# A new table of steps for a fused RWKV-5 and squared-ReLU FFN kernel: seven loads issued by ScalarE's queue, two more chunks transposed on TensorE

## The chip, the cores and the metric

The kernel runs on one core of one Trainium2 chip. The metric is the device time of one execution in microseconds, lower is better. Three runs of the kernel before took 174.09, 176.03 and 176.28 us (median 176.03 us). One further execution was recorded by the hardware profiler; every line of profile below comes from it.

## The reference

Two layers follow each other. The first is a linear attention with a decayed state, per batch `b` (4) and head `h` (8), over 768 time steps, with heads of width 48; the second is a feed-forward layer on the 3072 rows of width 384 that come out of it.

```python
for t in range(S):
    kt, vt, rt = (k[:, :, t].copy(), v[:, :, t].copy(), r[:, :, t].copy())
    cur = np.einsum('bhd,bhe->bhde', u[None] * kt, vt)
    y[:, :, t] = np.einsum('bhd,bhde->bhe', rt, state + cur)
    state = w[None, :, :, None] * state + np.einsum('bhd,bhe->bhde', kt, vt)
...
x = np.ascontiguousarray(attn_out.transpose(0, 2, 1, 3)).reshape(B * S, H * D)
h = np.maximum(x @ w_in, 0.0)          # w_in 384 x 2048
return (h * h @ w_out)                 # w_out 2048 x 384
```

All inputs and the output are float32 in HBM; the matmuls of the kernel work on bf16.

## The kernel before

**Tiling.** The 3072 rows are 24 chunks of 128 time steps; chunk `i` is batch `i % 4` and part `i // 4` of the sequence. Chunks 0 to 9, 22 and 23 go through the feed-forward layer one by one, the others in pairs (a "unit" `n` is one chunk or one pair; unit 15 is the last pair, 16 and 17 are chunks 22 and 23).

**Steps.** Each piece of work is a step with a short key, and a function `do_...` that issues its instructions:

- `Lr`, `Lk`, `Lv` + chunk (line 313): one DMA of 192 KB that loads r, k or v of the chunk. `wrow`, `urow` (263, 266) load the small rows w and u.
- `ln`, `bw`, `exk`, `ext`, `wt`, `wl`, `bu`, `ub` (274 to 302) make the powers of the decay, `Wkhat` and `Wt2`, once. `wlm` (304) spreads the last of them.
- `kh`, `rt` (327, 330) scale k and r; `P0`, `P`, `du`, `dv` (333 to 353) make the term with u; `vb` (355) casts v to bf16.
- `Tk`, `Tr` (371, 374): four TensorE transposes each of the scaled k and r, evicted by `ek`, `er` (377, 380). From chunk 5 on one DMA transpose `T` (383) on SyncE's queue does the work of both.
- `A` (388): 8 matmuls of scores; `M` (404): mask and eviction; `Y` (414): 8 matmuls, and 4 more against the state from chunk 4 on; `U`, `S` (431, 446): state update; `xs`, `X`, `xT` (441, 452, 459): sum, transpose (3 matmuls) and eviction into the layout of the feed-forward layer.
- `W1_q`, `W2_q` (476): one DMA of 768 KB for a quarter `q` of `w_in` or `w_out`. It goes into one of 5 float32 staging tiles and is cast to bf16 by `C1_q`, `C2_q` (484). `W2_3` alone is issued by GpSimd's queue, with the cast in the DMA.
- `F n_s` (489): 12 matmuls (6 of twice the width for a pair) of hidden units; `F n_q` of a single chunk needs quarter `q` of `w_in`. `R`, `Q` (506, 512): relu, then square. `G i_q` (523): 4 matmuls of output that need quarter `q` of `w_out`. `os`, `st` (541, 554): eviction and store.

**Order.** A table, `ORDER` (line 25), the written-out result of a search, lists all 915 steps as `key:engine`, with P for TensorE, A for ScalarE, D for VectorE, G for GpSimd, S for SyncE, and behind P the numbers of the PSUM banks. `Plan.run` (117) reads it, and the loop at line 575 issues the steps in this order. The scheduler is switched off (`tc.manual_schedule()`), so each engine runs its own steps strictly in the order in which the table lists them, and waits only for data, tiles and banks. All loads and all weight quarters but `W2_3` are issued by SyncE. `preload_act_table_set` (205) is ScalarE's first instruction. `PE_T` (17) is a constant that no other line reads; the number of chunks transposed on TensorE follows from the table.

In the table before, SyncE's list begins: `Lr0 wrow Lr1 Lk0 Lk1 urow Lr2 Lk2 Lk3 Lr3 Lv1 Lv0 Lv2 W1_0 W1_1 Lv3 Lk4 Lr4 W1_2 W1_3 Lv4 Lk5 Lr5 W2_0 W2_1 Lv5 Lk6 T5 W2_2 Lr6 Lr7 Lk7`. TensorE's list around the first output steps reads: `... F2_2 F1_3 F4_1 F4_3 U4 F4_0 G0_0 G3_0 G2_0 G3_1 G0_1 A5 F4_2 G1_0 G2_1 U5 Y5 G1_1 G4_0 G1_2 G2_2 X5 G3_2 ...`. `C2_0` and `C2_1` are cast by GpSimd, `C2_2` by ScalarE.

Of the kernel before, what the change touches and what calls it, by code (L numbers as in the profile page):

```python
# [25 lines left out]
Lr0:S wrow:S ln:A bw:P0 exk:A ext:A Lr1:S Lk0:S Lk1:S P00:D P01:D wt:P1 wl:A kh0:D kh1:D rt0:D  # L26
urow:S Lr2:S bu:P0 ub:A Tk0:P1 ek0:A Lk2:S kh2:D Tr0:P2 rt1:D Lk3:S P02:D kh3:D rt2:D er0:A Tk2:P0
Tr1:P1 er1:A Tk1:P2 ek1:A ek2:A A0:P34 Tk3:P1 A1:P25 Tr2:P0 Lr3:S Lv1:S Lv0:S vb0:A ek3:A vb1:A
er2:A P0:D M0:D du0:D M1:D rt3:G P1:G Lv2:S W1_0:S du1:D Tr3:P6 er3:A vb2:A C1_0:A W1_1:S Lv3:S
Lk4:S Lr4:S W1_2:S W1_3:S Lv4:S Lk5:S Lr5:S W2_0:S W2_1:S Lv5:S Lk6:S dv0:G P03:G dv1:G Y0:P3  # L30
xs0:D U0:P4 U1:P1 A2:P07 M2:D Y1:P2 A3:P56 X0:P3 xs1:D X1:P0 xT0:A F0_0:P2 wlm:D P2:G P3:G du2:D
du3:D dv2:G xT1:A F1_0:P0 Y2:P3 C1_1:A dv3:G kh4:G rt4:G vb3:A F1_1:P7 R1_0:A R0_0:A M3:D Y3:P5
xs2:D U3:P0 U2:P6 X2:P3 F0_1:P2 S1:D xs3:D xT2:D X3:P5 Tk4:P1 S0:D F2_1:P3 Tr4:P4 xT3:D S2:D S3:D
er4:D ek4:D F3_0:P5 F2_0:P6 F3_1:P0 Q1_0:A R1_1:A Q1_1:G P04:G P4:G R0_1:A Q0_1:D A4:P14 Q0_0:A
C1_2:A F0_2:P7 F3_2:P2 R3_0:A Q3_0:D M4:D du4:D W2_3:G dv4:G kh5:G rt5:G T5:S C1_3:A F3_3:P5
F2_3:P1 R3_1:A vb4:A Y4:P4 Q3_1:D R3_2:A Q3_2:D F0_3:P0 F1_2:P2 xs4:D X4:P4 R2_0:A R2_3:A Q2_0:D
R2_1:A R0_2:A Q2_3:A xT4:A Q2_1:D F2_2:P1 W2_2:S R2_2:A R3_3:A Q0_2:A Q3_3:D F1_3:P6 R0_3:A Q2_2:A
Q0_3:A F4_1:P4 vb5:A R4_1:A R1_3:A F4_3:P1 R4_3:A Q4_1:A R1_2:A C2_0:G U4:P3 F4_0:P7 S4:D G0_0:P0
G3_0:P5 G2_0:P3 C2_1:G G3_1:P G0_1:P A5:P16 M5:D F4_2:P4 G1_0:P2 G2_1:P R4_0:A Q1_2:A Q4_0:A
C2_2:A P05:G kh6:G P5:G du5:D dv5:D Lr6:S rt6:G U5:P1 Y5:P6 xs5:D S5:D G1_1:P G4_0:P7 G1_2:P  # L40
G2_2:P Lr7:S Lk7:S X5:P1 G3_2:P G2_3:P Q1_3:A R4_2:A Q4_3:A os2:A xT5:D F5_0:P1 G3_3:P os3:A
G0_2:P Lr8:S Lv6:S vb6:A F5_1:P3 T6:S A6:P54 Lk8:S rt7:G kh7:G T7:S rt8:D P06:D P6:D du6:D P07:G
kh8:G dv6:G M6:D G0_3:P os0:D G4_1:P F5_3:P6 R5_1:A R5_0:A Q5_0:A Y6:P4 P08:D xs6:D U6:P0 A7:P51
F5_2:P3 X6:P4 G1_3:P Q4_2:A G4_2:P M7:D G5_0:P1 Lv7:S vb7:A xT6:A Y7:P4 Lk9:S Lr9:S T8:S F6_0:P5
G4_3:P P7:G du7:D P8:G du8:D kh9:G dv7:D xs7:D X7:P4 rt9:G P09:D Q5_1:A os1:A R5_3:A Q5_3:A G5_1:P
A8:P62 S6:D M8:D Lv9:S Lv8:S Lr11:S Lk11:S Lr10:S R6_0:A xT7:A P9:G Q6_0:G R5_2:A F6_2:P4 R6_2:A
F6_3:P3 R6_3:A Q5_2:A vb8:A F7_2:P0 U7:P4 F7_3:P2 R7_3:A F7_0:P3 Q6_3:A R7_0:A G5_2:P Y8:P2 du9:D
dv8:D S7:D xs8:D F7_1:P4 F6_1:P3 X8:P2 xT8:D Lk10:S G5_3:P T9:S G6_0:P6 A9:P25 Q6_2:A vb9:A R6_1:A
Q7_3:A Q6_1:A st0:S Lr12:S Lv10:S rt10:G kh10:G T10:S rt11:G st1:S Lk12:S F8_2:P3 Q7_0:A R7_1:A
R7_2:A G6_1:P P010:D kh11:D M9:D F8_1:P4 Y9:P0 U9:P2 F8_3:P5 R8_2:A Q7_2:A R8_1:A Q7_1:A G6_2:P  # L50
G7_0:P3 vb10:A os5:A P10:D dv9:G du10:D xs9:D X9:P0 xT9:A R8_3:A T11:S Q8_2:A F8_0:P1 G7_1:P
R8_0:A F9_2:P0 Lv11:S Lk14:S Lk13:S Lr13:S Lk15:S P011:G P11:G dv10:G os4:D Q8_1:D S9:D P012:D
rt12:G st2:S Lv12:S st3:S kh12:G P12:G T12:S du11:D dv11:G rt13:G kh13:G P013:G A10:P52 M10:D
A11:P47 M11:D R9_2:A F9_3:P1 F9_0:P0 G7_2:P vb11:A R9_3:A Q9_3:A Q8_3:A Q8_0:A U8:P1 F9_1:P2
R9_1:A R9_0:A Q9_0:A Y10:P4 S8:D xs10:D Y11:P7 xs11:D du12:D U11:P5 G7_3:P G6_3:P X10:P7 G8_0:P0
X11:P4 Q9_2:A xT10:A xT11:A S11:D G9_0:P2 U10:P7 P13:D S10:D kh14:G dv12:D du13:D G8_1:P F10_7:P4
F10_6:P5 F10_1:P7 T13:S Lr15:S R10_7:A kh15:G Q10_7:G rt15:G os7:A R10_1:A Q10_1:D Q9_1:A os6:D
F10_0:P4 F10_2:P3 G8_2:P G9_1:P R10_0:A R10_2:A vb12:A st5:S Lr14:S P014:G P14:G Lv13:S dv13:G
rt14:G Q10_2:D vb13:A A12:P64 A13:P71 M12:D M13:D R10_6:A Q10_6:A Q10_0:A G8_3:P G9_2:P F10_3:P3
R10_3:A Q10_3:A G9_3:P Y12:P5 Y13:P1 os9:D xs12:D F10_5:P7 G11_0:P2 xs13:D X13:P1 X12:P5 xT12:D  # L60
Lk16:S st4:S Lr17:S st7:S F10_4:P3 G10_0:P4 U12:P5 xT13:D F11_2:P1 F11_3:P6 R10_4:A R10_5:A
Q10_5:A R11_3:A Q10_4:A P015:G Lr16:S P016:D os8:D S12:D Q11_3:D du14:D rt16:G rt17:G P15:G du15:D
Lv15:S Lv14:S vb14:A T14:S T15:S F11_1:P0 U13:P5 F11_7:P7 R11_1:A G11_1:P vb15:A F11_0:P6 G11_2:P
G10_1:P R11_2:A Q11_2:A R11_0:A Lk17:S Lr18:S S13:D A14:P51 A15:P03 dv14:G P16:D kh16:G M14:D
dv15:G Q11_1:A R11_7:A G10_2:P U15:P6 G11_3:P F11_5:P1 M15:D F11_4:P5 Y15:P0 Q11_7:D os11:D
Q11_0:G kh17:G P017:G Y14:P3 xs14:D F11_6:P7 R11_6:A Q11_6:G G10_3:P X14:P3 U14:P2 xT14:A R11_5:A
R11_4:A xs15:D X15:P0 xT15:D du16:D G12_0:P7 G13_0:P3 F12_4:P1 G13_1:P F12_0:P5 Q11_4:A F12_1:P0
R12_0:A st6:S st9:S Lk18:S Lr19:S Lv16:S Lk19:S kh19:G T16:S Lk21:S os10:A rt18:G S15:D S14:D
rt19:D P17:D Q11_5:A R12_4:A vb16:A F12_3:P2 G12_1:P F12_2:P4 G12_2:P Q12_0:D kh18:G dv16:G T17:S
Lv17:S st8:S A17:P56 Q12_4:D du17:D R12_3:A R12_1:A Lk20:S Lr20:S T18:S T19:S Lr21:S P018:D dv17:G  # L70
P019:G kh20:G A16:P21 M16:D G13_2:P F12_5:P0 vb17:A R12_2:A U17:P4 G13_3:P U16:P1 F12_6:P2 Q12_3:A
R12_5:A Q12_5:G P18:G Q12_1:A Q12_2:A Y16:P0 M17:D xs16:D Y17:P5 xs17:D S16:D S17:D G15_0:P6
G12_3:P G14_0:P5 F12_7:P0 G14_1:P G15_1:P os12:D R12_7:A Q12_7:A R12_6:A Q12_6:A os13:A A19:P07
A18:P41 P020:G rt20:G G14_2:P G15_2:P xT16:S xT17:S F13_4:P2 R13_4:A F13_0:P3 R13_0:A Lv18:S
rt21:D M18:D M19:D du18:D kh21:G P19:G du19:D Lv19:S P021:G dv18:G dv19:D Q13_4:G P20:G vb18:A
vb19:A G14_3:P F13_3:P2 R13_3:A Q13_3:D F13_6:P3 U19:P0 Y19:P7 Y18:P1 xs18:D S19:D F13_1:P4
G15_3:P U18:P1 F13_5:P2 R13_1:A Q13_0:A Q13_1:A R13_5:A F13_2:P0 R13_2:A Q13_2:A F13_7:P4 G17_0:P2
G16_0:P0 S18:D xs19:D R13_6:A Q13_6:A T20:S T21:S st10:S st11:S os14:D os15:A G17_1:P A21:P35
A20:P71 Q13_5:G Lr22:S Lk22:S G17_2:P G16_1:P xT18:S xT19:S F14_1:P6 Lv20:S Lr23:S Lv21:S Lk23:S
P022:D rt22:D P22:G M20:D M21:D du20:D R14_1:A vb20:A R13_7:A F14_2:P1 F14_4:P7 R14_2:A vb21:A  # L80
Q13_7:D F14_0:P6 F14_3:P3 F14_6:P5 st12:S Lv22:S kh22:G P21:G T22:S st13:S R14_4:A Q14_1:A Y20:P4
Y21:P7 G16_2:P rt23:G kh23:G du21:D du22:D Q14_2:D dv20:D R14_0:A R14_3:A Q14_3:A Q14_4:A F14_5:P1
G17_3:P R14_5:A Q14_0:D G18_0:P6 G19_0:P3 Q14_5:A R14_6:A os17:A vb22:A T23:S dv21:G dv22:G P023:G
P23:G xs20:D xs21:D G18_1:P G19_1:P G18_2:P A22:P25 M22:D A23:P17 xT20:S Q14_6:A G16_3:P F14_7:P4
G19_2:P R14_7:A xT21:S F15_5:P2 F15_2:P4 st17:S Lv23:S vb23:A st14:S os16:D M23:D du23:D st16:S
F15_0:P1 F15_1:P7 Y22:P0 xs22:D R15_2:A Y23:P4 dv23:D xs23:D xT22:S xT23:S Q15_2:A Q14_7:A
F15_6:P5 G18_3:P R15_1:A R15_0:A os18:A R15_6:A Q15_6:G F15_4:P0 F15_3:P4 R15_3:A F15_7:P6 Q15_1:D
Q15_0:D G20_0:P1 G21_0:P4 G19_3:P Q15_3:A G20_1:P R15_5:A R15_4:A Q15_5:G F16_0:P0 F16_2:P2
F17_1:P5 F17_0:P7 R16_0:A Q16_0:D R15_7:A Q15_4:A Q15_7:D R17_0:A R17_1:A G21_1:P F17_2:P6
F16_1:P7 R16_1:A Q16_1:A F16_3:P5 R16_3:A Q16_3:A Q17_0:G Q17_1:G R16_2:A G21_2:P F17_3:P7 R17_3:A  # L90
G22_0:P0 G20_2:P G22_1:P G21_3:P G23_0:P7 Q16_2:A R17_2:A Q17_3:A G22_2:P G23_1:P Q17_2:G G22_3:P
# [50 lines left out]
def kernel(  # L142
# [62 lines left out]
    nc.scalar.preload_act_table_set("natural_log_exp_and_others")
# [416 lines left out]
```

## Time and profile before

| | us |
|---|---|
| median of 3 runs | 176.03 |
| the profiled execution, device time | 176.71 |
| its span, first to last instruction | 175.0 |
| TensorE busy | 162.5 (93%) |
| VectorE busy | 118.9 (68%) |
| ScalarE busy | 118.3 (68%) |
| GpSimd busy | 98.7 (56%) |

How to read it: busy time is the sum of an engine's instructions. A busy TensorE is not one at its peak, since a matmul's end is modelled and a matmul that waits behind another is counted too. Rows named SPq, ACTq or PEq are steps of an engine's instruction queue, among them the issue of a DMA; the transfer itself runs later, on the 16 DMA engines. "Landing" is the time from the start of the issue until all data has arrived. PEclk is the TensorE clock that was granted, as a share of full speed. In the timeline a bracket `[1.35 <-ACT hr L509]` says how long the engine sat idle before the row, and what ended that.

### The profile page before, as it was taken

How to read it: one execution, taken by the hardware profiler on the slowest of the kernel's cores; microseconds unless marked ns; L12 is line 12 of the kernel's file. 1: busy time of each engine (PE TensorE's matmuls, PEld its weight loads, DVE VectorE, ACT ScalarE, POOL GpSimd, SP SyncE). 2: the span in 40 equal slices, each digit the busy share in tenths (PEclk: the TensorE clock that was granted, in tenths of full speed). 3: DMA queues.
4: the chain of work that ended last, by engine and by line, in shares of the span. 5: the costliest groups of instructions: out<-in, count | busy, mean ns of one | idle time of the engine just before them, and what ended most of it. 6: DMA issues, size and time to landing. Idle time of an engine off the chain costs nothing.

```text
span 175.0 us, 4726 instructions
## 1 busy us (share of the span) xinstructions
PE 162.5 (93%) x1892; PEld 126.4 (72%) x1892; DVE 118.9 (68%) x223; ACT 118.3 (68%) x221; POOL 98.7 (56%) x114
## 2 busy tenths in 40 slices
PE   0997799996999999999999999999999899999991
...
PEclk9999579999999999999999999999999999999999
...
GB/s 90 199 189 326 229 324 198 297 202 203 203 179 195 167 170 181 205 182 227 182 244 198 152 223 190 202 173 54 233 176 48 226 209 136 70 90 22 71 4 180
DMA packets 105609, 30.85 MB, mean 176 GB/s; under 512 B 98802, under 2 KB 104052, under 8 KB 105588
## 3 DMA queue, kind: packets, MB, share of 16 engines
...
## 4 chain that ended last, share of the span: by engine, by line
PE 68%; DMA 14%; SPq 7%; ACT 4%; DVE 3%; issue 2%; POOL 1%; ACTq 0%; DVEq 0%
PE ps_O L530 31%; PE ps_H L496 28%; DMA Wf<-in_moe_w_out_dram 8%; SPq L315 6%; DMA Wf<-in_moe_w_in_dram 3%; PE ps_A L394 3%; DMA vf<-in_v_dram 2%; PE ps_Y L425 2%; ACT W L324 2%; PE ps_Y L420 2%; PE ps_U L435 2%; PE ps_X L456 1%; ACT hr L509 1%; POOL W L325 1%; DVE ps_U L449 1%
## 5 line engine op out<-in xcount | busy, mean ns | idle before, releaser
L496 PE MATMUL ps_H<-xT,W 128*128 128x128 bf16 (+1 forms) x864 | 74.2, 241 | 0.6 <-ACT xT L324 0.6
L509 ACT ACTIVATE hr<-ps_H 128x512 bf16<-128x512 f32 x96 | 54.6, 595 | 28.6 <-PE ps_H L496 26.8
L530 PE MATMUL ps_O<-W,hq 128*128 128x384 bf16 x384 | 71.0, 326 | 0.4 <-ACT W L324 0.4
L496 PEld LDWEIGHTS <-W 128*128 128x128 bf16 x864 | 62.7, 100 | 7.2 <-ACT W L324 0.5
L530 PEld LDWEIGHTS <-hq 128*128 128x128 bf16 x384 | 35.7, 98 | 19.9 <-issue 0.6
L408 DVE TENSOR_TENSOR Bm<-ps_A,maskJT 128x512 bf16<-128x512 f32 x48 | 30.3, 683 | 11.6 <-PE ps_A L394 11.5
L516 ACT ACTIVATE hq<-hr 128x512 bf16<-128x512 bf16 x61 | 37.1, 629 | 0.6
L331 POOL TENSOR_TENSOR rk<-rf,Wt 128x384 bf16<-128x384 f32 x17 | 16.9, 998 | 22.8 <-DMA rf<-in_r_dram 11.0
L518 POOL TENSOR_TENSOR hq<-hr 128x512 bf16<-128x512 bf16 x13 | 13.8, 1064 | 21.2 <-ACT hr L509 21.2
L328 POOL TENSOR_TENSOR rk<-kf,Wkhat 128x384 bf16<-128x384 f32 x19 | 19.0, 999 | 9.2 <-DMA kf<-in_k_dram 4.0
L520 DVE TENSOR_TENSOR hq<-hr,ps_H 128x512 bf16<-128x512 bf16 x22 | 14.7, 682 | 10.9 <-ACT hr L509 10.9
L339 POOL TENSOR_TENSOR P<-P,ub 128x384 f32<-128x384 f32 x18 | 17.9, 998 | 2.3 <-DVE P L336 1.1
L443 DVE TENSOR_TENSOR xs<-ps_Y,dv 128x384 bf16<-128x384 f32 x24 | 12.8, 552 | 7.3 <-PE ps_Y L425 6.8
L357 ACT CAST vb<-vf 128x384 bf16<-128x384 f32 x24 | 12.3, 515 | 8.1 <-DMA vf<-in_v_dram 8.1
L353 POOL TENSOR_TENSOR dv<-vf,du 128x384 f32<-128x384 f32 x17 | 14.0, 830 | 6.3 <-DVE P L339 2.6
L336 POOL TENSOR_TENSOR P<-rf,kf 128x384 f32<-128x384 f32 x13 | 13.0, 1000 | 2.1 <-DVE P L339 1.6
L343 DVE TENSOR_REDUCE du<-P 128x8 f32<-128x384 f32 x24 | 12.7, 544 | 0.1
L325 DVE COPY os<-ps_O 128x384 f32<-128x384 f32 x12 | 6.6, 551 | 8.7 <-PE ps_O L530 8.7
L450 DVE TENSOR_TENSOR S0W<-ps_U,WLm 128x384 bf16<-128x384 f32 x20 | 11.0, 556 | 0.6
L425 PE MATMUL ps_Y<-vb,Bm 128*128 128x48 bf16 x192 | 10.9, 186 | 0.0
L425 PEld LDWEIGHTS <-Bm 128*128 128x128 bf16 x192 | 9.7, 99 | 1.4 <-issue 0.8
L336 DVE TENSOR_TENSOR P<-rf,kf 128x384 f32<-128x384 f32 x11 | 7.8, 713 | 3.8 <-DMA kf<-in_k_dram 3.8
...
## 6 DMA issues: line engine op xcount, KB each, us to landing
...
rkT<-rk SPq DMA_TRANSPOSE x19, 3.9
```

The lines of the kernel that those rows point to most:

```text
L328: return engine(f"kh{i}").tensor_mul(rk_buf[i % NK][:, 1, :, 0:D], nat["k", i], Wkhat)
L331: return engine(f"rt{i}").tensor_mul(rk_buf[i % NK][:, 0, :, 0:D], nat["r", i], Wt2)
L336: return engine(f"P0{i}").tensor_mul(P0, nat["r", i], nat["k", i])
L339: return engine(f"P{i}").tensor_mul(P0s[i], P0s[i], ub)
L353: return engine(f"dv{i}").tensor_mul(dv, nat["v", i], du_b)
L408: nc.vector.tensor_mul(Bm[:, e], Ap[e], mask_b)
L425: nc.tensor.matmul(Y[:, hc, D * e : D * (e + 1)], Bm[:, e, hc, :], vb[:, 2 * hc + e, :], start=(c == 0), stop=True, skip_group_check=True,)
L496: nc.tensor.matmul(hp[:, fi, :], W1[s // size][:, c, 128 * f : 128 * (f + 1)], xTs[n][:, :, c, :], start=(c == 0), stop=(c == CCH - 1), sk ...
L509: nc.scalar.activation(hr, hp, AF.Relu)
L516: nc.scalar.square(hq, hr)
L520: nc.vector.tensor_mul(hq, hr, hp)
L530: nc.tensor.matmul(ps[f"O{i}"][:, 0:d_model], hsq[n, f // per][:, f % per, L * j : L * (j + 1)], W2[q][:, f % 4, :], start=(f == 0), stop= ...
```

## The change

The whole table of steps is replaced, and with it the queues of some steps:

- `Lk0`, `Lk1`, `Lk2`, `W1_2`, `W2_0`, `W2_1` and `W2_2` are listed under ScalarE: `queue(key)` issues their DMAs from ScalarE's queue, in the place that they have in ScalarE's list. `W1_0`, `W1_1`, `W1_3` and all other loads stay with SyncE.
- The load of the activation table moves from the head of the kernel to just before ScalarE's first step that is not a load, `ln`, behind the issue of `Lk0` to `Lk2`.
- The DMA transposes `T5` and `T6` are gone; `Tk5 Tr5 Tk6 Tr6` on TensorE and `ek5 er5 ek6 er6` on ScalarE and VectorE take their place. The table has 921 steps.
- `C2_2` moves from ScalarE to GpSimd. Of the 96 squares `Q`, GpSimd has 21 (before 13), ScalarE 55 (61), VectorE 20 (22). Some `P0`, `P`, `kh`, `rt`, `dv`, `xT`, `os` change between VectorE, GpSimd and ScalarE.

```diff
-PE_T = 5
+PE_T = 7
...
-    nc.scalar.preload_act_table_set("natural_log_exp_and_others")
...
+    def queue(key):
+        return nc.scalar if plan.eng[key] == "ACT" else nc.sync
...
-        inst = nc.sync.dma_start(out=t, in_=src[which][i % B, i // B])
+        inst = queue(f"L{which}{i}").dma_start(out=t, in_=src[which][i % B, i // B])
...
-        if plan.eng[f"W{a}_{q}"] == "SP":
+        if plan.eng[f"W{a}_{q}"] != "POOL":
             Wf[a, q] = stage.tile(shape, FP32, name=f"Wf{a}_{q}", tag="Wf")
-            return nc.sync.dma_start(out=Wf[a, q], in_=part)
+            return queue(f"W{a}_{q}").dma_start(out=Wf[a, q], in_=part)
...
+    tables = False
     for key in order:
+        if plan.eng[key] == "ACT" and key[0] not in "LW" and not tables:
+            nc.scalar.preload_act_table_set("natural_log_exp_and_others")
+            tables = True
```

The first part of the new table, in which all steps that are named later stand:

```
Lk0:A Lk1:A Lk2:A Lr0:S wrow:S ln:A bw:P0 exk:A ext:A P00:G urow:S Lr1:S Lr2:S Lv0:S Lv1:S Lk3:S
bu:P1 ub:A kh0:D wt:P2 Tk0:P1 kh1:D rt0:D P01:D rt1:D Lv2:S Lr3:S Tr0:P0 Tk1:P3 Tr1:P4 P0:D rt2:D
P1:D du0:D er0:A ek0:A vb0:A A0:P05 Tr2:P1 er1:A wl:A kh2:G dv0:G kh3:G U0:P4 vb1:A U1:P2 Tk2:P6
du1:D M0:D ek1:A ek2:D W1_1:S rt3:G vb2:A A1:P37 M1:D er2:A A2:P16 M2:D Y0:P0 xs0:D W1_0:S Lk5:S
Lv3:S W1_3:S Lr4:S Lk4:S Lr5:S W1_2:A Y1:P5 Tr3:P3 Tk3:P7 er3:A U2:P1 ek3:A X0:P0 A3:P73 Y2:P6
dv1:G xs1:D P02:G wlm:D xT0:D C1_1:A P03:G P2:G S0:D du2:D C1_0:A X1:P5 xT1:A F0_1:P0 R0_1:A vb3:A
F0_0:P4 R0_0:A Q0_0:A F1_0:P5 R1_0:A C1_3:A P3:G dv2:G S2:D M3:D xs2:D Y3:P3 X2:P6 U3:P7 F1_1:P4
...
F3_0:P2 R1_1:A Q0_3:A R3_3:A R1_3:A P04:G C1_2:A rt5:G Tr5:P6 F2_3:P7 er4:D A4:P01 Lv4:S vb4:A
er5:D A5:P65 F3_1:P3 R3_1:A Q3_3:A Q1_1:A Q3_1:A R3_0:A P4:G du4:D M4:D M5:D F1_2:P4 Y4:P0 Q1_3:G
dv4:G P05:G P5:G xs4:D F3_2:P3 F0_2:P1 R0_2:A X4:P0 xT4:D W2_0:A C2_0:G Lv5:S vb5:A Q3_0:A W2_1:A
U4:P5 F2_2:P6 R2_2:A S4:D Q0_2:G du5:D dv5:G F4_2:P0 F4_1:P1 Y5:P5 G0_0:P6 R2_3:A R1_2:A Q1_2:A
R3_2:A Q2_2:A Q2_3:D F4_0:P2 R4_0:A G3_0:P7 G1_0:P4 Q4_0:A xs5:D X5:P3 U5:P5 xT5:D C2_1:G G1_1:P
G0_1:P F4_3:P3 F5_1:P2 Q3_2:A R4_2:A Q4_2:A R4_3:A R4_1:A Lr7:S rt7:G Lr6:S rt6:D Lk6:S P06:G P6:G
S5:D Q4_3:D Lk7:S kh7:G W2_2:A F5_0:P5 G2_0:P0 G3_1:P F5_3:P3 Tr6:P1 R5_0:A Q4_1:A F5_2:P5 R5_3:A
er6:A R5_2:A Q5_0:A R5_1:A G2_1:P kh6:G Tk6:P1 C2_2:G G3_2:P G2_2:P G1_2:P Q5_1:A ek6:A Lr8:S
...
```

121 lines of the change are left out of this document (53 added, 68 removed).

## The prediction

> **What bounds the kernel now.** I read the page first, then the stretches, then the chain in order of time, then the timeline at the places where the chain leaves TensorE (PE). From the page: the span, PE's busy tenths, its clock, and the chain by line.
>
> ```profile
> span 175.0 us, 4726 instructions
> ...
> PE   0997799996999999999999999999999899999991
> ...
> PEclk9999579999999999999999999999999999999999
> ...
> PE ps_O L530 31%; PE ps_H L496 28%; DMA Wf<-in_moe_w_out_dram 8%; SPq L315 6%; DMA Wf<-in_moe_w_in_dram 3%; PE ps_A L394 3%; DMA vf<-in_v_dram 2%; PE ps_Y L425 2%; ACT W L324 2%; PE ps_Y L420 2%; PE ps_U L435 2%; PE ps_X L456 1%; ACT hr L509 1%; POOL W L325 1%; DVE ps_U L449 1%
> ```
>
> PE carries the chain, except where it waits for weight quarters. The stretches (start and end, length, busy us of PE, PEld, DVE, ACT, POOL, clock, DMA share, GB/s) say where:
>
> ```profile
> 14.20:17.60 3.40, 2.19 (x44) 1.58 (x42) 3.40 (x7) 2.75 (x6) 3.40 (x5) 1.00 1.02 375
> 17.60:21.00 3.40, 2.47 (x22) 2.31 (x23) 3.35 (x7) 3.40 (x5) 2.62 (x4) 0.51 1.19 229
> 21.00:24.40 3.40, 3.40 (x47) 3.40 (x45) 1.84 (x4) 2.43 (x5) 2.09 (x3) 0.50 0.88 283
> 38.10:41.50 3.40, 2.24 (x14) 1.24 (x13) 0.00 (x0) 1.84 (x4) 2.63 (x4) 1.00 1.10 145
> 50.00:150.00 100.00, 99.25 (x1167) 76.58 (x1165) 80.13 (x145) 69.21 (x135) 65.78 (x69) 1.00 0.91 181
> ```
>
> From 50 to 150 us PE is busy 99.25 of 100: nothing can be won there, and work that PE gets more is paid in full. The first 50 us decide. There the DMA engines are full (share about 1), and PE worked at half clock from 17.6 to 24.4, after a sparse stretch. The chain (start, length, what) and two timeline rows for the second gap:
>
> ```profile
> 11.24 5.86 DMA Wf<-in_moe_w_in_dram
> ...
> 19.03 2.72 PE ps_H L496 x24
> ...
> 37.22 1.48 POOL W L325
> 38.69 0.81 SPq L384
> ...
> 39.60 5.26 DMA Wf<-in_moe_w_out_dram
> 44.89 1.48 ACT W L324
> 46.42 1.46 PE ps_O L530 x8
> 47.88 0.17 PE ps_X L456 x3
> ...
> 49.34 0.67 PE ps_H L496 x12
> 50.01 1.30 PE ps_O L530 x8
> ...
> 63.11 0.17 PE ps_U L435 x4
> ```
>
> ```profile
> 33.56 5.94 SPq L384 DMA_TRANSPOSE rkT<-rk  x1
> ...
> 41.70 0.40 PE L394 MATMUL ps_A<-rkT 48*128 48x128 bf16 x8 [1.35 <-ACT hr L509]
> ...
> 46.42 1.46 PE L530 MATMUL ps_O<-W,hq 128*128 128x384 bf16 x8 [0.41 <-ACT W L324]
> ```
>
> The transpose T5 held SyncE's queue for 5.94 us, so W2_2 was issued only at 39.60. PE lost 1.5 us in front of A5 (1.35 in the row; with the modelled end of the matmul before it taken off, 1.5) and 0.6 in front of G1_2 (0.41 in its row, likewise): 2.1 us.
>
> **The change part by part.** Durations are those of the chain above: F 0.67, one G 0.65, U 0.17, three transposes 0.17.
>
> *T5, T6 become 16 transposes on PE.* 16 x 0.17/3 = +0.9 us, paid in full. Their four evictions run on ACT and DVE, which are not full (69 and 80 of 100). With T5 goes its wait, and W2_2 no longer stands behind it on SP: the 2.1 us above go. What is late next is counted below.
>
> *The start.* In the timeline the activation table, wrow, ln and the first weights:
>
> ```profile
> 0.81 1.28 ACT L205 ACT_TABLE_LOAD   x1 [0.81 <-PEq L606]
> ...
> 1.32 0.45 SPq L264 DMA_DIRECT2D wrow<-in_w_dram  x1
> ...
> 2.27 2.04 SPq L315 DMA_DIRECT2D kf<-in_k_dram  x2
> ...
> 3.60 0.52 ACT L275 ACTIVATE lrow<-wrow 1x384 f32<-1x384 f32 x1 [1.52 <-DMA wrow<-in_w_dram]
> ...
> 11.24 1.53 SPq L480 DMA_DIRECT2D Wf<-in_moe_w_in_dram  x2
> ...
> 17.13 1.47 ACT L324 CAST W<-Wf 128x1536 bf16<-128x1536 f32 x1 [0.65 <-DMA Wf<-in_moe_w_in_dram]
> ```
>
> Three issues on ACT ahead of the table: at 0.45 each it is loaded by 0.81 + 1.35 + 1.28 = 3.4, still under the wait for wrow that ends at 3.60. At 1.02 each (half of the 2.04) ln starts 1.5 late, but the first F waits for a weight that lands at 17.1, so this costs nothing; that cover goes only if the weights come over 1 us earlier. Two queues fill the engines sooner: at most 0.9 us, one 192 KB load of the eleven issued between 0.81 and 11.24. Against it: W1_1 still stands behind eleven loads, and ACT issues W1_2 right behind er2, that is when Lv2, the tenth of the eleven, has landed (vb2 stands ahead of it). Both quarters then share the engines; another 0.79 MB at the 375 GB/s of the first stretch is 2.1 us, for a quarter that is first needed after twelve F. F starts later by 2.1 - 0.9 = +1.2 (ends -0.9 and +2.1). I leave the half clock there as it is.
>
> *W2_0, the main term.* On ACT it stands directly behind R0_2, which waits for F0_2. An issue behind a waiting step has no row, but a step of ACT's own queue has, in the chain at 139 us:
>
> ```profile
> 134.84 4.18 DMA vf<-in_v_dram
> ...
> 139.04 0.02 ACT vb L357
> ...
> 139.16 0.02 ACTq L509
> ```
>
> Lv21 landed at 134.84 + 4.18 = 139.02, vb21 began, and only then did ACT's queue go on to a relu. So I take it that ACT's queue does not pass a waiting step, and W2_0 is issued 0.1 us after F0_2's end. Then 5.26 for the transfer and 1.48 for the cast by POOL, both from the chain: G0_0 can start 6.85 after F0_2. PE has in its list between them X4, U4, F2_2, F4_2, F4_1, Y5. Y by its first row and the next step's:
>
> ```profile
> 54.23 0.21 PE L420 MATMUL ps_Y<-S0W,rkT 128*128 128x96 bf16 x1
> ...
> 54.60 0.33 PE L435 MATMUL ps_U<-vb,rk 128*128 128x96 bf16 x4
> ```
>
> 0.17 + 0.17 + 3 x 0.67 + 0.37 = 2.7. PE stands still for 6.85 - 2.7 = 4.2 us (4.15). For the transfer, the landing times of the weight tile (first 60 us), and of r:
>
> ```profile
> DMA to landing us min/median/max: 5.3/6.7/8.9
> ...
> DMA to landing us min/median/max: 2.8/4.5/7.2
> ```
>
> Ends: 0.79 MB against r's 0.2 adds 0.59 MB, 1.6 us at 375 GB/s, to the fastest r, 2.8: 4.4, a stall of 3.3. At the median 6.7: 5.6. I take 5.26, since SP's loads have mostly run by then.
>
> *The clock after it.* A stretch with 2.19 of 3.40 busy was followed by two at half clock; one with 2.24, at 38.10, was not. A stall of 4.2 leaves under 1 busy in one of them, so I expect the clock to halve. If it does so at the stall's end, PE works at half speed for the rest of that stretch and one full one: about 5 us, +2.5 (0 to 3.4).
>
> *W2_1* is issued right behind W2_0; on POOL C2_0, Q0_2, dv5 stand ahead of C2_1, and PE has 3.0 us of work until G1_1. At half clock this is hidden, at full clock 0.4.
>
> *W2_2* on ACT stands behind R4_3, R4_1, which wait for F4_3: 0.3 + 5.26 + 1.48 = 7.0 until G3_2. PE has four F, three G, Tr6, Tk6: 2.7 + 2.0 + 0.5 = 5.1. Stall 1.9 (ends 1.0 at 4.4, 3.4 at 6.7).
>
> *The rest.* POOL gains eight squares:
>
> ```profile
> L518 POOL TENSOR_TENSOR hq<-hr 128x512 bf16<-128x512 bf16 x13 | 13.8, 1064 | 21.2 <-ACT hr L509 21.2
> ```
>
> 8 x 1.06 = 8.5 us on an engine busy 66 of 100; ACT loses six. Behind C2_0 on POOL wait Q0_2 and dv5, with PE waiting anyway. SP's later loads move up past the four weights, and their users have slack. Nothing.
>
> *Sum:* 0.9 - 2.1 + 1.2 + 4.2 + 2.5 + 1.9 = +8.6 us. The sum is made on the profiled execution's 176.7 (span 175.0 and 1.7 around it), 0.7 above the median of 176.03: 185.3, and 184.6 as a median.
>
> **The rivals.** *First, not slower: ACT's queue runs ahead.* If a DMA on ACT's queue passes relus and squares that still wait, W2_0 is issued up to six steps earlier (R3_1, Q3_3, Q1_1, Q3_1, R3_0, R0_2), 6 x 0.6 = 3.6 us by the rows of ACT:
>
> ```profile
> L509 ACT ACTIVATE hr<-ps_H 128x512 bf16<-128x512 f32 x96 | 54.6, 595 | 28.6 <-PE ps_H L496 26.8 <-DVE xT L325 1.4
> L516 ACT ACTIVATE hq<-hr 128x512 bf16<-128x512 bf16 x61 | 37.1, 629 | 0.6
> ```
>
> The first stall falls to 0.6, the clock stays, the last stall goes: 0.9 - 2.1 + 1.2 + 0.6 = +0.6, median 176.6. It decides from two steps on: 1.2 us less stall is what the clock may turn on. Against it speak the rows at 139 us, for it none. The Trainium skill ("Perfetto Trace Analysis", section "DVE / Act Engine Instruction") states that the sequencer is free for the next instruction once one is pushed into the wait queue, before its semaphores are satisfied. By that rule this rival would hold; the rows at 139 us do not agree with it for a queue step behind a waiting cast, and no run here yet shows it for a DMA issue. 17 in 100.
>
> *Second, slower still: the two queues block each other's issue.* The transpose's issue took 5.94 us and the two of kf 2.04; if an issue on ACT waits for such a one on SP, W2_0 and W2_2 come later by some 1.5 us each (between the 1.02 of one kf and half of the 5.94, nearer the first): +3, 187.6. For it: SP issues loads in this stretch. Against it: most of them are short by then. The Trainium skill (the same page, section "DMA Instruction — HWDGE") says that the descriptor generator is locked for one sequencer at a time; no row here shows two queues at once. 12 in 100.
>
> *Third, faster:* the first rival with a start that keeps its full clock. Of the work between 17.6 and 24.4 half of the 5.4 us from 19.03 on is given back (2.7), and the start gains 0.9 instead of losing 1.2: 176.6 - 2.7 - 2.1 = 171.8. For it: two queues at the start. Against it: the eleven loads and the sparse stretch are the same. 6 in 100.
>
> **How the numbers follow.** The forecast, 65 in 100, is 184.6; its own range, from the ends above and with or without the loss of clock, is 181 to 189. With the rivals the range is 176.5 to 189.5: outside it lie the third rival, half of the first and a few cases above. A measurement of this kernel tells about 2% from no change, 172.5 to 179.6 being the same. Slower: 65 + 12 = 77 in 100; same: 17; faster: 6.
>
> **What would show it.** Right: in the profile after, a DMA of w_out on ACTq that starts just when the last matmul of F0_2 ends; POOL's cast idle before it for that DMA; PE idle about 4 us before the first ps_O row, near 38 to 43 us; PEclk at 5 in the slices behind it; a second gap of 1 to 3 us before G3_2. No DMA transpose on SP before 45 us. W1_1's cast some 1 us later than 17.13. Wrong: w_out issues on ACTq ahead of the relus, and G0_0 near 38 us without a gap; or a first F well before 19 us at full clock.

## The result and the profile after

The changed kernel takes 186.12 us (median of four runs, 185.34 to 186.42) against 175.58 us for the kernel before on the same chip (174.09 to 176.28): a ratio of 1.0606, 95% interval 1.0565 to 1.0648. It is slower, by 10.5 us. Of the two profiled executions, the one after has a span of 184.6 us and the one before 175.0, so 9.6 us are to be found; the other 0.9 comes from the profiled execution of the kernel before, which was 1.1 us above its median, the one after only 0.2.

The page of the profile after (lines numbered 2 higher than before): span, TensorE's busy tenths, its granted clock and the DMA engines' share in slices of 4.6 us, the group of the output matmuls with its idle time, and the median landing time of the quarters of `w_out` that ScalarE's queue issues.

```profile
span 184.6 us, 4747 instructions
...
PE   0899897952994999999999999999999999999992
...
PEclk9999999995799999999999999999999999999999
DMA  6999999993049994999989999495495895524004
...
L532 PE MATMUL ps_O<-W,hq 128*128 128x384 bf16 x384 | 71.6, 329 | 8.2 <-POOL W L327 8.2
...
Wf<-in_moe_w_out_dram ACTq DMA_DIRECT2D x3, 768.0 KB, 6.6
```

TensorE has one deep hole, in the slices from 37 to 46 us, and a shallower one near 57. The output matmuls waited 8.2 us for weights cast by GpSimd, all in these two places. The DMA digits 0 and 4 right behind the first hole are as telling: the transfer engines stood idle there while a weight quarter was still to come. The stretches (columns as before: length, busy us of PE, PEld, DVE, ACT, POOL, clock, DMA share, GB/s):

```profile
20.00:25.00 5.00, 4.74 (x56) 4.32 (x54) 3.55 (x8) 3.41 (x6) 3.25 (x5) 1.00 1.13 276
...
40.00:45.00 5.00, 0.09 (x1) 0.08 (x1) 0.69 (x1) 1.12 (x3) 1.60 (x2) 0.64 0.71 247
45.00:50.00 5.00, 5.00 (x35) 3.37 (x35) 1.08 (x3) 3.34 (x6) 4.01 (x4) 0.68 0.00 0
...
60.00:150.00 90.00, 90.00 (x1046) 69.00 (x1045) 73.13 (x137) 56.94 (x113) 58.51 (x62) 1.00 0.92 170
```

Between 40 and 45 us TensorE did nothing, from 45 to 50 it worked at a clock of 0.68 and no byte moved, and from 60 to 150 us it was never idle. (The 1.00 of the first of these stretches is no measured clock: see the last section.) The timeline at the first hole: the last matmuls of F0_2, the issues of W2_0 and W2_1, the cast C2_0 and the first output step G0_0.

```profile
35.80 0.83 PE L498 MATMUL ps_H<-xT,W 128*128 128x128 bf16 x12
36.76 0.38 ACTq L482 DMA_DIRECT2D Wf<-in_moe_w_out_dram  x1
...
37.23 1.59 ACTq L482 DMA_DIRECT2D Wf<-in_moe_w_out_dram  x1
43.40 1.46 POOL L327 CAST W<-Wf 128x1536 bf16<-128x1536 f32 x1 [6.82 <-DMA Wf<-in_moe_w_out_dram]
44.91 1.44 PE L532 MATMUL ps_O<-W,hq 128*128 128x384 bf16 x4 [5.56 <-POOL W L327]
```

F0_2 ended at 36.63, W2_0 was issued 0.13 us later, its cast could begin 6.64 us after that, and G0_0 followed the cast. The bracket of 5.56 us is the whole hole. The second one, with W2_2, has the same build:

```profile
51.63 0.39 ACTq L482 DMA_DIRECT2D Wf<-in_moe_w_out_dram  x1
...
57.81 1.46 POOL L327 CAST W<-Wf 128x1536 bf16<-128x1536 f32 x1 [3.45 <-DMA Wf<-in_moe_w_out_dram]
...
59.33 0.97 PE L532 MATMUL ps_O<-W,hq 128*128 128x384 bf16 x5 [2.67 <-POOL W L327]
```

Two smaller rows of the profile after were in no step of the prediction. The first is the transpose Tr5, which waited for the scaled r of chunk 5 (rt5), and that for its load:

```profile
30.81 0.99 POOL L333 TENSOR_TENSOR rk<-rf,Wt 128x384 bf16<-128x384 f32 x1 [1.45 <-DMA rf<-in_r_dram]
...
31.86 0.40 PE L365 MATMUL ps_Tr<-identity,rk 128*128 128x128 bf16 x4 [1.15 <-POOL rk L333]
```

The second is a wait that is gone. In the profile before, the chain at 139 us that the prediction quotes ended in this row of TensorE, which has no counterpart after:

```profile
140.10 0.20 PE L420 MATMUL ps_Y<-S0W,rkT 128*128 128x96 bf16 x1 [0.75 <-ACT hr L509]
```

### The profile page after: what moved, and what is told of

It is laid out like the page before. It is cut to its first block, busy times and chain, and to the rows that moved or that the text cites. A ratio compares the mean times of both kernels' runs of the same rounds, so it can differ in the third digit from the quotient of the medians.

```text
span 184.6 us, 4747 instructions
## 1 busy us (share of the span) xinstructions
PE 165.2 (89%) x1908; PEld 129.0 (70%) x1908; DVE 117.6 (64%) x228; ACT 113.1 (61%) x213; POOL 106.2 (57%) x121
## 4 chain that ended last, share of the span: by engine, by line
PE 66%; DVE 0%; ACT 0%; issue 0%; POOL 0%
PE ps_O L532 31%; PE ps_H L498 26%; PE ps_A L396 3%; PE ps_Y L427 2%; PE ps_Y L422 2%; PE ps_U L437 1%; PE ps_X L458 1%; DVE oh L553 0%; ACT os L546 0%; POOL P L338 0%
## 5 line engine op out<-in xcount | busy, mean ns | idle before, releaser
L518 ACT ACTIVATE hq<-hr 128x512 bf16<-128x512 bf16 x55 | 33.6, 633 | 0.4
L520 POOL TENSOR_TENSOR hq<-hr 128x512 bf16<-128x512 bf16 x21 | 21.9, 1053 | 13.8 <-ACT hr L511 13.8
L333 POOL TENSOR_TENSOR rk<-rf,Wt 128x384 bf16<-128x384 f32 x15 | 15.0, 998 | 12.8 <-DMA rf<-in_r_dram 9.6
L338 POOL TENSOR_TENSOR P<-rf,kf 128x384 f32<-128x384 f32 x18 | 18.3, 1018 | 6.6 <-issue 1.8
L330 POOL TENSOR_TENSOR rk<-kf,Wkhat 128x384 bf16<-128x384 f32 x15 | 14.9, 999 | 12.2 <-DVE P L341 5.4
L522 DVE TENSOR_TENSOR hq<-hr,ps_H 128x512 bf16<-128x512 bf16 x20 | 13.5, 682 | 10.6 <-ACT hr L511 10.6
L341 POOL TENSOR_TENSOR P<-P,ub 128x384 f32<-128x384 f32 x15 | 15.3, 1020 | 8.2 <-DVE P L341 6.0
L355 POOL TENSOR_TENSOR dv<-vf,du 128x384 f32<-128x384 f32 x19 | 15.6, 828 | 4.0 <-DVE du L345 3.9
L327 DVE COPY os<-ps_O 128x384 f32<-128x384 f32 x11 | 5.9, 550 | 9.1 <-PE ps_O L532 9.1
L326 ACT COPY os<-ps_O 128x384 f32<-128x384 f32 x12 | 5.8, 481 | 8.0 <-PE ps_O L532 8.0
```

The source lines that it names most:

```text
L330: return engine(f"kh{i}").tensor_mul(rk_buf[i % NK][:, 1, :, 0:D], nat["k", i], Wkhat)
L333: return engine(f"rt{i}").tensor_mul(rk_buf[i % NK][:, 0, :, 0:D], nat["r", i], Wt2)
L338: return engine(f"P0{i}").tensor_mul(P0, nat["r", i], nat["k", i])
L341: return engine(f"P{i}").tensor_mul(P0s[i], P0s[i], ub)
L355: return engine(f"dv{i}").tensor_mul(dv, nat["v", i], du_b)
L518: nc.scalar.square(hq, hr)
```

## The experiments

Twelve kernels were run. The theory: W2_0 and W2_2 are issued too late, because each stands in ScalarE's list behind a step that waits for a late F; TensorE runs dry, and its clock halves after the first stop. It is the place in the list that costs, not the queue itself. The rivals: ScalarE's queue as such is to blame, or ScalarE's queue runs ahead of waiting steps and the loads are late for another reason, or the halved clock or the loads of the other queue carry the larger part. Times of the kernel before in the same runs: 175.09 us beside the first four, 175.62 beside the next four, 175.03 beside the three after those, 175.27 beside the last. The line numbers differ by a few from kernel to kernel.

**1. The three quarters of `w_out` back on SyncE, in the new table.**

```diff
-... Lr5:S W1_2:A ... xT4:D W2_0:A C2_0:G Lv5:S vb5:A Q3_0:A W2_1:A ... kh7:G W2_2:A
+... Lr5:S W2_0:S W1_2:A ... C1_3:A W2_1:S ... xT4:D C2_0:G Lv5:S W2_2:S vb5:A Q3_0:A ... kh7:G
```

> W2_0 and W2_1 go back to SyncE's queue behind Lr5, W2_2 behind Lv5; the rest of the new table stays. Theory (the quarters are late because their issue stands behind relus that wait for PE): they are issued near 26 to 31 us, G0_0 starts without its 5.7 us gap, G3_2 without its 2.8 us gap, and the clock does not halve at 44.9; 186.1 - 5.7 - 2.8 - 1.5 = 176.1, at most 1.5 more where the loads behind them come later. Rival (SyncE's queue is so full that the quarters come late there too): a gap stays in front of G0_0, 180 or more.

Measured: 177.93 us (177.59 to 179.89), ratio 1.0198 (1.0128 to 1.0269). Both holes are gone and the clock is whole from 25 us on, so the late quarters carry most of the loss: of the 10.5 us over the kernel before, 2.8 are left. That is 1.8 us more than the 176.1 expected. What is left of TensorE's waits in the loops:

```profile
PE ps_A L395 <- ACT rkT L325: 2.5, 2, 2.2
PE ps_Y L426 <- ACT vb L358: 1.3, 1, 1.3
```

These are a wait near 18 us, where ScalarE stood at the issue of W1_2 until W1_0 had landed, and one for the late load Lv4.

```profile
18.70 0.37 ACTq L481 DMA_DIRECT2D Wf<-in_moe_w_in_dram  x1
19.11 0.59 ACT L325 COPY rkT<-ps_Tr 128x512 bf16<-128x512 bf16 x1 [4.76 <-DMA Wf<-in_moe_w_in_dram]
```

Both belong to this run and not to the changed kernel, in which W1_2 was issued at 13.33 us and TensorE waited 0.2 us for casts of v: W2_0, put in front of W1_2, gave that issue another landing to wait for (the next run shows how), and W2_0 and W2_1 stand in front of Lv4. So this run does not tell what the rest of the new table costs.

**2. The quarters on ScalarE, but early in its list.**

```diff
-... W2_0:A (behind xT4) ... W2_1:A (behind Q3_0) ... W2_2:A (behind kh7)
+... W2_0:A (behind C1_3) ... W2_1:A (behind R2_0) ... W2_2:A (behind C1_2)
```

> The three quarters stay on ScalarE's queue, but earlier in its list: W2_0 behind C1_3, W2_1 behind R2_0, W2_2 behind C1_2. Theory (the place in ScalarE's list counts, not the queue): issued near 26, 27 and 31 us, both gaps go, 176 to 178. Rival (a weight quarter on ScalarE's queue is slow, or blocks ScalarE's steps, wherever it stands): over 181. If ScalarE's queue ran ahead of waiting steps, the issue would come before C1_3 has begun.

Measured: 182.96 us (182.77 to 183.76), ratio 1.0472 (1.0429 to 1.0514). This missed: it is early in the list and still slow. The chain in order of time around the new hole, and ScalarE's longest waits:

```profile
25.41 8.97 DMA vf<-in_v_dram
...
34.40 0.38 ACTq L481
...
34.88 0.61 ACT hr L510
...
35.53 1.44 PE ps_H L497 x12
```

```profile
ACT hr L510 <- DMA vf<-in_v_dram: 7.1, 1, 7.1
```

No relu needs v. The issue of W2_1 waited for the landing of Lv4, a load that SyncE had issued, and held ScalarE and the relus behind it for 7.1 us. The waits written into the program tell why: every load, on SyncE's or ScalarE's queue, reports its landing on one of eight counters in turn, and an issue waits until the load that used its counter last has landed. W2_1 came to the counter of Lv4. So a load on ScalarE's queue can stop ScalarE for a load of another queue. The theory stands for the first hole, but "early" is not enough: the neighbours in the turn count as well.

**3. W2_0 one relu later.**

```diff
-R0_2:A X4:P0 xT4:D W2_0:A C2_0:G Lv5:S vb5:A Q3_0:A W2_1:A U4:P5 F2_2:P6 R2_2:A S4:D
+R0_2:A X4:P0 xT4:D Lv5:S vb5:A Q3_0:A U4:P5 F2_2:P6 R2_2:A W2_0:A W2_1:A C2_0:G S4:D
```

> W2_0 and W2_1 stand one relu later in ScalarE's list, behind R2_2 instead of R0_2; C2_0 moves with them in the table but keeps its place on GpSimd. F2_2 ends 1.0 us after F0_2 (X4, U4 and 12 matmuls between). Theory (the issue follows the end of the F that the relu in front of it waits for): issue at F2_2's end + 0.1, the gap in front of G0_0 grows by 1.0 to about 6.7 us, 187.1 in all. Rival (ScalarE's queue runs ahead of waiting steps, or the DMA engines set the landing): no change, 186.1.

Measured: 185.14 us (184.91 to 187.31), ratio 1.0615 (1.0540 to 1.0690).

```profile
37.72 0.93 ACTq L481 DMA_DIRECT2D Wf<-in_moe_w_out_dram  x2
...
43.89 1.44 PE L531 MATMUL ps_O<-W,hq 128*128 128x384 bf16 x4 [4.58 <-POOL W L326]
```

By the time alone this run missed the 187.1 expected: against the kernel before it stands where the changed kernel does (1.0606), which is what the rival said. The rows decide. The issue moved from 36.76 to 37.72, 0.96 us later, with the relu in front of it. That refutes a queue that runs ahead: it follows the relu that it stands behind. But the quarter was ready sooner: the cast began at 42.38, 4.7 us after the issue instead of 6.6, so G0_0 came 1.0 us earlier. How long a quarter takes depends on what else is under way, and that was not in the theory.

**4. The old table with one late quarter.** Only W2_0 is put on ScalarE, behind R2_2; all else is the kernel before.

```diff
-Lr5:S W2_0:S W2_1:S ... W2_2:S R2_2:A R3_3:A
+Lr5:S W2_1:S ... W2_2:S R2_2:A W2_0:A R3_3:A
```

> The old table in the new code; only W2_0 moves, from SyncE to ScalarE's list behind R2_2. R2_2 started at 34.28 in the profile of before and G0_0 at 36.93. Theory (one quarter behind one waiting relu is enough): issue at 34.3, landing 5.3 to 6.6 us later, cast 1.5: G0_0 at 41.1 to 42.4, a gap of 4.2 to 5.5 us, and the clock may halve behind it (+1.5); part of it hides the two gaps that followed (2.1). 175.6 + 3.5 to 6, so 179 to 181.6. Rival (it needs the new table's other moves too): under 177.5.

Measured: 180.73 us (180.13 to 183.20), ratio 1.0317 (1.0260 to 1.0374), in the range expected. R2_2 and the issue of W2_0 behind it, TensorE's longest wait, and the stretch behind that:

```profile
33.18 0.60 ACT L509 ACTIVATE hr<-ps_H 128x512 bf16<-128x512 f32 x1
33.19 0.42 ACTq L480 DMA_DIRECT2D Wf<-in_moe_w_out_dram  x1
```

```profile
PE ps_O L530 <- POOL W L325: 5.4, 1, 5.4
```

```profile
40.00:45.00 5.00, 3.60 (x12) 1.75 (x12) 0.00 (x0) 2.70 (x4) 5.00 (x5) 0.50 1.24 269
```

One moved step makes the hole of 5.4 us and the clock of 0.50 behind it, in a table that has nothing else of the change.

**5. TensorE kept busy in the hole.** The changed kernel, with 20 matmuls of 512 columns ahead of G0_0 whose results nobody reads.

```diff
+if i == 0 and q == 0:
+    fill = psum.tile([128, 512], FP32, name="ps_fill", tag=f"b{plan.banks['O0'][0]}")
+    for _ in range(20):
+        nc.tensor.matmul(fill, identity, W1[1][:, 0, :], start=True, stop=True, skip_group_check=True)
```

> The changed kernel with 20 extra matmuls of 512 columns in front of G0_0, into the bank that G0_0 then starts afresh; nothing reads them. They run for about 4.3 us of the 5.7 us gap. Theory (the half clock from 41.4 to 48.2 comes from the idle gap and costs PE half of the 3.3 us after 44.9): the clock stays whole, 186.1 - 1.5 = 184.6. Rival (the slow stretch behind the gap is that of W2_1 and its cast, and the clock is incidental): 186.1, with a gap in front of G1_1 instead.

Measured: 183.37 us (183.22 to 183.44), ratio 1.0456 (1.0421 to 1.0491), 2.75 us under the changed kernel. In the profiled execution the clock stays at 1.0 from 22.5 us on, so it was the idle time that had halved it. The clock gives back 1.6 us (5 us at 0.68, the row above); as much came unexpected from the second hole (2.67 to 1.02), and a wait of 1.0 us for a cast of v, 0.2 in the changed kernel, took some of it back. W2_2 was issued 1.5 us earlier and could be cast 4.5 us after its issue, not 6.2:

```profile
50.12 0.38 ACTq L481 DMA_DIRECT2D Wf<-in_moe_w_out_dram  x1
54.66 1.46 POOL L326 CAST W<-Wf 128x1536 bf16<-128x1536 f32 x1 [1.33 <-DMA Wf<-in_moe_w_out_dram]
56.17 3.41 PE L535 MATMUL ps_O<-W,hq 128*128 128x384 bf16 x20 [1.02 <-POOL W L326]
```

**6. SyncE's loads of chunks 6 and 8 held back.** T7, which waits for its input until about 53 us, is put ahead of Lr8, Lk8 and Lv6, so that these do not share the engines with W2_0.

```diff
-Lk7:S kh7:G W2_2:A ... Lr8:S ... Lk8:S Lv6:S T7:S A7:P12
+Lk7:S kh7:G T7:S W2_2:A ... Lr8:S ... Lk8:S Lv6:S A7:P12
```

> T7 moves in SyncE's list in front of Lr8, Lk8, Lv6, which so are issued after about 54 us and not at 33.5 to 36.5. Theory (W2_0 took 6.6 us to land, not 5.3, because these three loads were still in flight, as the later issue that landed sooner in the run with one relu later suggests): W2_0 lands 1.5 to 2 us sooner, near 41.5, and the gap shrinks by as much: 184.3, if chunk 8 is not late in its turn. Rival (two quarters in flight share the engines, whatever else runs): the gap stays, 186.1.

Measured: 186.26 us (184.59 to 188.65), ratio 1.0588 (1.0505 to 1.0670): no gain in the median. The four executions lie far apart, though: two, at a mean granted clock of 0.99, took 184.59 and 185.16 us, near the 184.3 expected, and two, at 0.97 and 0.96, took 187.36 (the profiled one) and 188.65.

```profile
41.76 1.46 POOL L326 CAST W<-Wf 128x1536 bf16<-128x1536 f32 x1 [4.76 <-DMA Wf<-in_moe_w_out_dram]
43.28 1.44 PE L531 MATMUL ps_O<-W,hq 128*128 128x384 bf16 x4 [3.54 <-POOL W L326]
...
58.65 3.79 PE L531 MATMUL ps_O<-W,hq 128*128 128x384 bf16 x12 [2.64 <-POOL W L326]
```

```profile
45.00:50.00 5.00, 5.00 (x33) 3.16 (x31) 1.72 (x4) 3.23 (x6) 2.63 (x4) 0.64 0.00 2
...
55.00:60.00 5.00, 2.36 (x16) 1.30 (x14) 0.41 (x1) 2.96 (x6) 2.42 (x2) 0.88 1.34 158
60.00:65.00 5.00, 5.00 (x37) 2.67 (x36) 1.83 (x5) 0.89 (x2) 3.59 (x4) 0.78 1.45 187
```

The first hole shrank by 2.0 us, from 5.56 to 3.54, as expected: those loads are what had stretched W2_0's transfer. Now they run beside W2_2, and the second hole stayed at 2.6 us. What the first hole gave, the clock took back in this execution: TensorE started again at 43.28 us and worked at half speed to 48.6 (0.64 from 45 to 50), which is 2.0 us of work more at half speed than in the changed kernel and so 1.0 us lost, and the clock fell a second time behind the second hole (0.88 and 0.78), for 3.4 us of work, 1.7 us lost. Why it fell there, and not behind the equal second hole of the changed kernel, stays open.

**7. All four quarters on SyncE.** As the first run, and W1_2 too, behind W1_3.

```diff
-... W1_3:S Lr4:S Lk4:S Lr5:S W1_2:A
+... W1_3:S W1_2:S Lr4:S Lk4:S Lr5:S W2_0:S
```

> All weight quarters but W2_3 back on SyncE's queue: W1_2 behind W1_3, W2_0 and W2_1 behind Lr5, W2_2 behind Lv5. In the run with W2 alone moved back, ScalarE's queue stood still until 18.7, because the issue of W1_2 waited for the landing of W1_0, whose semaphore it shares, and PE idled 2.5 us at 17.7. Theory (an issue on ScalarE waits for an earlier load's landing, and holds the steps behind it): that gap goes, 177.9 - 1.8 = 176.1. Rival (the gap came from the loads themselves being late): 177.9.

Measured: 179.52 us (178.27 to 180.46), ratio 1.0231 (1.0165 to 1.0296), not the 176.1 expected. The wait near 18 us went, as theory said, but in a single queue the loads behind the quarters became late: TensorE waited 1.66 us for rt5 (Tr5; 1.15 in the changed kernel) and 1.51 us for vb4 (0.2).

```profile
32.48 0.40 PE L364 MATMUL ps_Tr<-identity,rk 128*128 128x128 bf16 x4 [1.66 <-POOL rk L332]
...
37.10 0.21 PE L426 MATMUL ps_Y<-vb,Bm 128*128 128x48 bf16 x2 [1.51 <-ACT vb L358]
```

**8. The quarters on ScalarE, in places whose turn is free.** W2_0 behind C1_3, W2_1 behind R3_1, W2_2 behind R0_2.

```diff
-... W2_0:A (behind xT4) ... W2_1:A (behind Q3_0) ... W2_2:A (behind kh7)
+... W2_0:A (behind C1_3) ... W2_1:A (behind R3_1) ... W2_2:A (behind R0_2)
```

> The quarters on ScalarE's queue again: W2_0 behind C1_3, W2_1 behind R3_1, W2_2 behind R0_2. In the run with W2_1 behind R2_0 its issue waited until 34.4 for the landing of Lv4, and ScalarE stood still for 7 us. Here W2_1 shares its semaphore with a load that should have landed by about 36. Theory (place and shared semaphores, not the queue): no gap over 1.5 us in front of G0_0 or F0_3, 177 to 179. Rival (quarters on ScalarE cost by themselves): over 181.

Measured: 178.68 us (178.54 to 178.95), ratio 1.0189 (1.0159 to 1.0219), level with the first run, with the clock whole and no wait of TensorE behind its start above 1.0 us:

```profile
PE ps_H L497 <- ACT W L325: 1.0, 1, 1.0
```

ScalarE's queue is thus as good as SyncE's here, if the places are right. That settles queue against place. It is still 3.1 us over the kernel before beside it, with no single wait to blame; where that lies was not followed up.

**9 to 12. A version of the old table.** None of the first eight runs beat the kernel before, so the last four leave the quarters where it has them. What the change took away rightly are the waits around T5. These runs keep the old table and put T5 on TensorE; the later three move a few more steps.

```diff
-rt5:G T5:S C1_3:A ... F4_3:P1 ... U4:P3 F4_0:P7 S4:D
+rt5:G C1_3:A ... F4_3:P1 Tk5:P2 ek5:D ... U4:P3 F4_0:P7 Tr5:P2 S4:D er5:D
```

> The old table, with one part of the change alone: chunk 5's DMA transpose T5 becomes eight transposes on PE (Tk5, Tr5 behind F4_3 and F4_0, evictions by DVE); all loads, and vb5, stay where they were. The prediction put both gaps of the old kernel, 1.5 us before A5 and 0.6 before G1_2, down to T5. Its reading gives 8 x 0.057 = +0.45 and -2.1: 1.65 us less than the kernel before, about 173.9, with A5 near 40.3 us. Rival: before A5 the last releaser was R4_3's relu, which stands on ScalarE behind vb5, which waits for Lv5's landing at 39.6; T5's landing at 41.33 was only level with it. Then the gap before A5 stays at 1.0 to 1.5 us, W2_2's alone goes, and the time is -0.6 + 0.45 = -0.1, that of the kernel before.

Measured: 182.16 us (181.36 to 182.96), ratio 1.0415 (1.0377 to 1.0453): far off both theories, through a place that was badly chosen. Bank P2 belongs to F1_2 at that time, whose relu R1_2 is late:

```profile
41.69 0.59 PE L364 MATMUL ps_Tk<-identity,rk 128*128 128x128 bf16 x4 [6.62 <-ACT hr L510]
```

The next run only moves a cast on ScalarE, `vb5`, from in front of R4_1 to behind R4_3.

> As the run before, and vb5 moved on ScalarE behind R4_3, so that the relus before A5 no longer wait for Lv5. If Lv5 held A5, this run loses the gap before A5 and is 1.2 to 1.5 us faster than the run before, about 1.65 us under the kernel before (173.9). If T5 alone held it, both runs are equal.

Measured: 180.29 us (179.56 to 181.81), ratio 1.0316 (1.0267 to 1.0365), 1.9 us under the run before; TensorE's wait fell by 1.8:

```profile
PE ps_Tk L364 <- ACT hr L510: 4.8, 1, 4.8
```

So a cast that waits for a load (Lv5) holds up the relus behind it and through them TensorE. The third moves two steps at 139 us as well (vb21 behind R14_4, Y21 behind G16_2).

> As the run before, and the gap of 0.9 us at 139 us taken out in the same manner: vb21 behind R14_4 on ScalarE, Y21 behind G16_2 on PE. 0.7 to 0.9 us faster than the run before, about 173.1, 1.5% under the kernel before. Rival: Y21's result is needed soon, and the wait goes to xs21 and xT21 behind it; then equal to the run before.

Measured: 179.71 us (179.08 to 182.08), ratio 1.0269 (1.0233 to 1.0305). The 0.6 us to the run before lie inside the two intervals; with the hole ahead of it, it tells nothing about the steps at 139 us. The last run mends the place:

```diff
-rt5:G T5:S C1_3:A ... Q0_2:A Q3_3:D F1_3:P6 R0_3:A ... vb5:A R4_1:A ... R4_3:A Q4_1:A
+rt5:G C1_3:A ... Q0_2:A F1_3:P6 Tk5:P3 Tr5:P7 ek5:D er5:D Q3_3:D R0_3:A ... R4_1:A ... R4_3:A vb5:A Q4_1:A
```

> As the run before (T5 on PE, vb5 behind R4_3, the steps at 139 us moved), but Tk5 and Tr5 stand behind F1_3 in the banks P3 and P7, which are free there, and their evictions stand ahead of Q3_3 on DVE. In the three runs before Tk5 waited 4.8 to 6.6 us for R1_2, since bank P2 is that of F1_2, not of F3_2: a place chosen wrongly, no cost of the transposes. With it mended the gaps of 1.5, 0.6 and 0.9 us of the old kernel go, and eight transposes add 0.45: 2.5 us under the kernel before, about 172.6, 1.4%. Rival: the gap before A5 stays (Lv5 lands late by some other way, or G0_0's quarters do): 0.9 + 0.6 - 0.45 = 1.0 us under the kernel before, about 174.

Measured: 174.27 us (median of twelve, 173.73 to 175.17) against 175.27 (of seventeen), ratio 0.9943 (0.9918 to 0.9969). It beats both kernels, by 0.6% and 6%. TensorE's longest waits in its profile are all at the start:

```profile
PE ps_bw L269 <- ACT lrow L273: 4.3, 1, 4.3
PE ps_H L497 <- ACT xT L325: 1.3, 1, 1.3
```

Its span is 172.3 us, 2.7 below that of the kernel before, which is what was expected; the medians differ by 1.0 only, not by the 2.5 expected. By its time alone the run came out at the rival's 174; its profile, with no wait left before A5, does not show the rival's gap. The profiled execution of the kernel before (176.71 us) was at the upper end of that kernel's runs, 1.4 us above this median, so part of the waits in its profile is less in other executions. Which part stays open. Open too is which of the two held A5, T5 or the relus behind vb5, since the last run takes away both.

## Why the prediction was right, and where it was not

It gave 184.6 us, slower; 186.12 was measured. The errors of its terms run from -0.9 to +1.5 us and largely cancel, so that the sum came within 1.0 us is in part luck; that TensorE runs dry in the two places it named is not. The terms, with the waits of TensorE taken from the rows above (0.15 us added to each bracket for the modelled end of the matmul before it, as the prediction did):

| term | predicted | measured |
|---|---|---|
| W2_0: hole before G0_0 | +4.2 | +5.7 |
| half clock behind it | +2.5 | +1.6 (5 us at 0.68) |
| W2_2: hole before G3_2 | +1.9 | +2.8 |
| W2_1 | hidden | hidden |
| waits around T5 | -2.1 | -2.1 |
| 16 transposes | +0.9 | +0.9 (by the count; not measured alone) |
| start | +1.2 | +0.3 (fourth F at 24.76, before 24.43) |
| Tr5 waits for rt5 | none | +1.3 |
| wait at 139 us | none | -0.9 |
| sum | +8.6 | +9.6 (span) |

**The mechanism of the main term was right.** The issue followed F0_2's end by 0.13 us (predicted 0.1), the cast took 1.46, TensorE had the work that was counted, and it ran dry where it was said. Runs 3 and 4 show that the issue goes with the relu in front of it and that this one step makes the hole. The Trainium skill ("Perfetto Trace Analysis", section "DVE / Act Engine Instruction") frees the sequencer once an instruction is in the wait queue. By that rule the first rival would have held. W2_0 in the changed kernel and in run 3 does not test it: there the relu's wait for TensorE is a step of the queue by itself (in the changed kernel's trace at 36.67 us), and the issue stands behind that step. Run 4 tests it. There R2_2 carries its wait itself, W2_0's issue behind it has no wait of its own, and the queue's step in front of R2_2 was over at 32.69 us; F2_2's last result was there at 33.16, R2_2 began at 33.18, and W2_0 was issued at 33.19, half a microsecond later than a free queue could have issued it. So this trace does not bear the rule out for an issue behind a waiting relu.

**Mis-sized: W2_0's transfer.** The step "I take 5.26, since SP's loads have mostly run by then" failed. W2_0 could be cast 6.64 us after its issue; SP's loads of chunks 6 and 8 had been issued just before (run 6: 4.6 us without them). The step's upper end, 6.7, was the better reading. W2_2 took 6.2. SyncE's T7 and loads, issued from 53.44 us on, 1.8 us behind W2_2, ran beside it; in run 5 they came 2.3 us behind it and it took 4.5, but in run 3, again at 1.8, it took 5.2. So what stretched W2_2 is not shown.

**Mis-sized: the clock.** It fell at the place named, but already during the hole: a clock of 0.64 from 40 to 45 us is 3.6 of the 5 us at half speed. Half speed lasted for another 3.2 us of work (0.68 from 45 to 50), a loss of 1.6; that it would begin "at the stall's end" was wrong. Run 5 shows that the idle time caused it.

**Wrong: the start.** The predicted reason, that W1_1 shares the engines with W1_2 and lands later, did not happen: W1_1 landed 5.8 us after its issue at 10.72, at 16.5, before the 17.1 of the first quarter of the kernel before. The first F came 0.7 us later (19.76 against 19.03) for two other reasons: the cast of W1_1 began at 17.72 us (17.13 before), since ScalarE was evicting rkT until then, and xT0, which held F for the last 0.47 us, stood on VectorE behind the two copies of wlm.

```profile
17.83 1.49 DVE L307 COPY WLm<-wlt 48x192 f32<-48x192 f32 x2
19.35 0.36 DVE L327 COPY xT<-ps_X 128x384 bf16<-128x384 bf16 x1
...
19.76 1.44 PE L498 MATMUL ps_H<-xT,W 128*128 128x128 bf16 x12 [0.47 <-DVE xT L327]
```

Part of this was made up: the fourth F, the first one at full speed in either kernel, began at 24.76 us (last section) against 24.43 before.

```profile
24.43 0.86 PE L496 MATMUL ps_H<-xT,W 128*128 128x128 bf16 x12
```

The costs of the table load and of ln were hidden as said. The new order of ScalarE's and VectorE's steps ahead of the first F had not been followed.

**Missing: Tr5 and the wait at 139 us.** "SP's later loads move up past the four weights, and their users have slack. Nothing." failed for chunk 5: before, T5's result was first needed at 41.7 us, and after, A5 stands at 33.1, so Lr5 had no slack any more. A step that is taken to another engine was costed at its own duration, but it also came 8 us earlier in TensorE's list. And "nothing can be won there" held for 99.25 of 100 us: the other 0.75 was won. Together the two leave 0.4 us.

**The rivals.** The first is refuted by the issues of runs 3 and 4. The second, that two queues block each other's issue, did not cost anything: W2_0 and W2_2 were issued in 0.38 and 0.39 us, with no issue of SP under way. Where two do meet, these rows speak against it, in which an issue on ACT takes 0.37 us in the midst of one on SP that takes 2.93:

```profile
12.81 2.93 SPq L317 DMA_DIRECT2D vf<-in_v_dram  x1
13.33 0.37 ACTq L482 DMA_DIRECT2D Wf<-in_moe_w_in_dram  x1
```

The Trainium skill's lock of the descriptor generator (the same page, section "DMA Instruction — HWDGE") costs nothing that shows in these rows. The queues do block each other, but in another way, that of run 2; in the changed kernel the longest issue on ScalarE's queue around the holes is the 1.59 us of W2_1, whose landing counter was free; what it stood at is not shown. The third rival fell with the first; both kernels reach full speed at about 24.4 us (last section).
